# A gated mix of a long convolution and dilated attention: spectra regrouped in fours, inputs in transform rows, transposes on TensorE

## The chip, the cores and the metric

The kernel runs on one core of a Trainium2 chip. The metric is device time in microseconds (us) of one execution, lower is better. The engines are TensorE (PE in the profile; PEld are its weight loads), VectorE (DVE), ScalarE (ACT), GpSimd (POOL) and SyncE (SP). SP issues nearly all DMAs, in order, on one queue. A row "SPq" or "ACTq" of the profile is the issuing of a DMA on that engine's queue.

## The reference

The inputs are bf16: x, k, v of 2048 positions by 640 channels, and weights. The output mixes two branches by a gate per position.

```python
x = A_q
g = _sigmoid((x * gate_w).sum(-1, keepdims=True))
a = _A_ref(x, A_k, A_v, A_shift_k, A_ssm_k, A_ssm_D)
b = _B_ref(x, B_wqkv, B_wo)
return g * a + (1 - g) * b
```

Branch a convolves k with four taps per channel, multiplies by v (this is kv), convolves kv with a filter per channel as long as the sequence (`ssm_k`, by an FFT of length 4096), adds `kv * ssm_D` and multiplies by x. Branch b projects x to queries, keys and values of 32 heads of 20, attends from each position to the eight positions at distances 0, 2, ... 14 before it, and projects by `wo`.

## The kernel before, in words

All positions are split by parity into two halves of 1024, since the attention's distances are even. Branch b works on 18 blocks (9 a half) of 114 queries and 121 keys; a mask is added to the scores by 11 extra rows of the keys and queries, so a block's scores are a plain matmul, and an exponential on ScalarE makes the weights.

The order of the instructions on every engine comes from a planner (`Plan`, L149), which runs when the kernel is built. Each part of the kernel is a generator that asks for an engine with a cost in ns and the events it needs (`Req`); the planner starts whatever could start first, with 120 ns of handicap for each unit of the part's priority (the second argument of `plan.add`, L886 to L907). The costs and due times only fix the order; on the chip the engines wait on semaphores. Four pairs of PSUM banks are handed out by the planner (`take=1`). The helper `copy` (L273) empties PSUM on ScalarE (L275) or VectorE (L277), as the planner chooses.

The parts, in the order in which they matter:

- Loads (`loads`, L347): four DMAs that transpose x into `xT` (L355, channels on partitions), the weights of value, query and key, the taps, k and v in rows of 16 positions per partition (`kin`, `vin`), later `wo` and the filter `h_lin`.
- Value projection (`vproj`, L472) into `VW`, 18 units of 10 matmuls; query and key projection (`qkproj`, L516), 30 units into two staging tiles `stg`. `fragger` (L551) copies heads out of the staging tiles into three rotating sets `kb`, `qb` of four heads each, by 64 DMAs on SP (L573).
- Scores and weights (`score_gen`, L585; exponential at L604 into `ETall`) and the products with the values (`pv_gen`, L610), normalised by VectorE into `oS`.
- The short convolution (`conv`, L437): four taps and the product with v on VectorE, 4 positions of a partition at a time. Its result is written to DRAM (`kv_out`, L393), and read back (`kv_back`, L701) as `kvT`, which has 64 consecutive positions of 160 channels on each partition, the layout that the transform wants.
- The gate (`gate`, L492): 80 matmuls of one column, an exponential, then VectorE, then a write of 2048 numbers to DRAM (`g_scr`, L506) and four reads that turn them into `g_nat` (L509).
- The long convolution as a two-step transform (`transform`, L708): 10 first-step units (`s1_unit`, L649) and 11 second-step units (`s2_unit`, L669), each emptied by `copy`, in place. It is run for the filter (`h`) and for kv (`u`), each in two halves of 80 of the 160 channels of a partition group (P = 0, 1). In a spectrum tile the 40 channels of a group are innermost. A swapped copy `Hw` of the filter's spectrum (`swaps`, L740) lets VectorE form the complex product by two multiplications (`mults`, L756). `inverse1` (L773) is the first step back, 160 matmuls a half, into `Cm`.
- `outproj` (L794) turns `oS` (5 units of transposes), then multiplies by `wo` (16 units) and scales by 1 - g into `bl`.
- x is loaded again in rows (`late_loads`, L826), scaled by g on VectorE (`qscale`, L840), and `final` (L847) does the last step of the inverse in six rounds of up to 96 matmuls, multiplies, adds `bl` and stores.

Space decides much of the order. The second half of u takes the space of `oT`, so it follows the output projection (`ev("outproj")`, L735). `G`, the constants of the second step, takes the space of half of v, so it is loaded when the convolution and its writes are done (L402 to L407). `ETall` shares space with the taps (L309), so it waits for the first block of the convolution.

Of the kernel before, what the change touches and what calls it, by code (L numbers as in the profile page):

```python
# [10 lines left out]
BF = mybir.dt.bfloat16  # L11
# [22 lines left out]
XW = X0 + 2 * HS + 16  # L34
# [10 lines left out]
CR = 4  # L45
RES = 16
# [59 lines left out]
def ccol(sb):  # L106
    return X0 + 128 * sb


# [32 lines left out]
LEAN_QK = 600.0  # L142
LEAN_V = 0.0
LEAN_H = 0.0
# [103 lines left out]
def kernel(  # L248
# [39 lines left out]
    Wv = p0.tile([128, NDT, D], BF, name="Wv", tag="wo")  # L288
    kin = p0.tile([128, 16, D], BF, name="kin", tag="H")
    h_lin = p0.tile([128, 80, 2, 64], BF, name="h_lin", tag="kv")  # L290
# [3 lines left out]
    dpool = ctx.enter_context(tc.tile_pool(name="scratch_dram", bufs=1, space=DRAM))  # L294
    kv_d = dpool.tile([S, D], BF, name="kv_d")
    g_scr = dpool.tile([S], F32, name="g_scr")
    g_pos = p0.tile([128, 16], F32, name="g_pos")
    g_nat = p0.tile([128, 16], F32, name="g_nat")
    omg = p0.tile([128, 16], F32, name="omg")

# [8 lines left out]
    early = pR.tile([128, 3 * D + 4 * D], BF, name="early", tag="ET")  # L309
    halo = early[:, 0:3 * D].rearrange("p (n c) -> p n c", n=3)  # L310
    wraw = early[:, 3 * D:7 * D].rearrange("p (c j) -> p c j", j=4)
# [8 lines left out]
    pa = pL.tile([128, CR, D], BF, name="pa")  # L320
    pb = pL.tile([128, CR, D], BF, name="pb")
    wl = pL.tile([128, 4, D], BF, name="wl")
    mm = pL.tile([128, BK + BQ], BF, name="mm")
    Dz = pL.tile([128, 160], BF, name="Dz")
    wg = pL.tile([128, NDT], BF, name="wg")
# [17 lines left out]
    st = {"vin": [None, None]}  # L343

    def loads():  # L347
        def load(name, dst, src, us, deps=(), bg=None):
            g = yield Req("S", 500.0, deps, move=us, bg=bg, pri=None if bg is None else 1)
            nc.sync.dma_start(dst, src)  # L350
            mark(name, g)

        def load_x(c):
            g = yield Req("S", 500.0, (), move=2600.0)
            nc.sync.dma_start_transpose(xT[:, :, X0 + 512 * c:X0 + 512 * c + 512],  # L355
                                        raw(x2, (1024 * (c % 2) + c // 2) * D, [[2 * D, 512], [1, D]]))
            mark(f"x{c}", g)

        def load_rows(name, dst, src, r0, r1, deps=(), bg=1500.0):
            yield from load(name, dst, raw(src, r0 * D, [[16 * D, 128], [1, (r1 - r0) * D]]), (r1 - r0) * 128 * 1280 / 250.0, deps, bg)  # L360

        def load_k(a):
            yield from load_rows(f"k{a}", kin[:, 8 * a:8 * a + 8, :].rearrange("p n c -> p (n c)"), k2, 8 * a, 8 * a + 8)

        def load_v(a):
            v_ = p0.tile([128, 8, D], BF, name="vin", tag=("oS", "G")[a])
            st["vin"][a] = v_
            yield from load_rows(f"v{a}", v_[:].rearrange("p n c -> p (n c)"), v2, 8 * a, 8 * a + 8, ())

        yield from load_x(0)  # L370
        yield from load("Wv", Wv[:], W3[:, :, 2, :], 2600.0)
        yield from load_x(1)
        yield from load("W0", Wqk[:, :, 0, :], W3[:, :, 0, :], 2600.0)
        yield from load_x(2)
        yield from load("W1", Wqk[:, :, 1, :], W3[:, :, 1, :], 2600.0)
        yield from load_x(3)
        yield from load("wraw", wraw.rearrange("p c j -> p (c j)"), raw(A_shift_k, 0, [[0, 128], [1, 4 * D]]), 2200.0)
        for a, b in ((1, 113), (113, 128)):
            yield from load(f"halo{a}", halo[a:b].rearrange("p n c -> p (n c)"), raw(k2, (16 * a - 3) * D, [[16 * D, b - a], [1, 3 * D]]), 900.0)
        yield from load_k(0)  # L380
        yield from load_v(0)
        yield from load_k(1)
        yield from load_v(1)
        yield from load("ident", ident[:], ca["ident"].ap(), 200.0)
        wo = p0.tile([128, NDT, D], BF, name="wo", tag="wo")
        st["wo"] = wo
        yield from load("wo", wo[:], B_wo.rearrange("(t p) n -> p t n", p=128), 2400.0, [ev("vproj")], 1500.0)
        for c in range(2):
            for q in range(4):
                yield from load(f"h{q}{c}", h_lin[32 * q:32 * q + 32, :, c, :],  # L390
                                raw(A_ssm_k, (160 * q + 80 * c) * S, [[64, 32], [S, 80], [1, 64]]), 2100.0, (), 1500.0)

    def kv_out():  # L393
        for a in range(16 // CR):
            n = CR * a
            g = yield Req("S", 500.0, [ev(f"conv{a}")], move=2600.0)
            nc.sync.dma_start(raw(kv_d[0:1, 0:1], n * D, [[16 * D, 128], [1, CR * D]]),
                              st["vin"][n // 8][:, n % 8:n % 8 + CR, :].rearrange("p n c -> p (n c)"))
            mark(f"kvD{a}", g)

    def load_G():
        yield Req("S", 1.0, [ev("conv")])  # L402
# [7 lines left out]
    def heads():  # L410
        for c0, c1 in ((0, X0), (X0 + 2 * HS, XW)):
            nc.gpsimd.memset(xT[:, :, c0:c1], 0.0)
# [526 lines left out]
```

## Time and profile before

| | us |
|---|---|
| median of 3 runs | 282.11 |
| lowest and highest | 281.13, 284.21 |
| span of the profiled execution, first to last instruction | 280.1 |
| PE, DVE, ACT, POOL busy in it | 224.8, 175.6, 169.0, 20.2 |
| instructions | 8105 |

The profile is of one execution. Its own time is its span plus what lies before the first and after the last instruction, which the trace does not show; the median of the runs is 2.0 us above the span. A busy PE is not a PE at its full rate, as its matmuls overlap. 39.9 MB are moved by DMA. The convolution's last product on VectorE starts at 87.3 us, the last query/key unit at 131.7 and the last scores' exponential at about 155 us.

### The profile page before, as it was taken

How to read it: one execution, taken by the hardware profiler on the slowest of the kernel's cores; microseconds unless marked ns; L12 is line 12 of the kernel's file. 1: busy time of each engine (PE TensorE's matmuls, PEld its weight loads, DVE VectorE, ACT ScalarE, POOL GpSimd, SP SyncE). 2: the span in 40 equal slices, each digit the busy share in tenths (PEclk: the TensorE clock that was granted, in tenths of full speed). 3: DMA queues.
4: the chain of work that ended last, by engine and by line, in shares of the span. 5: the costliest groups of instructions: out<-in, count | busy, mean ns of one | idle time of the engine just before them, and what ended most of it. 6: DMA issues, size and time to landing. Idle time of an engine off the chain costs nothing.

```text
span 280.1 us, 8105 instructions
## 1 busy us (share of the span) xinstructions
PE 224.8 (80%) x3622; PEld 179.5 (64%) x3626; DVE 175.6 (63%) x186; ACT 169.0 (60%) x204; POOL 20.2 (7%) x23
## 2 busy tenths in 40 slices
PE   0699999699696985599899878989999979498420
PEld 0589787477454654456667867878977768398320
DVE  0012699999989533437787799999204266970682
ACT  1034256844877065368889798965765597166760
POOL 9940020000000000100000000000000000000000
PEclk9999999899877797579655799997999997779755
DMA  8999862976788438665699779000699940000275
GB/s 158 265 260 281 245 231 55 327 268 139 186 178 190 93 42 121 117 175 148 159 147 146 89 167 209 5 2 2 122 196 223 216 148 2 0 2 0 64 175 147
DMA packets 62857, 39.93 MB, mean 143 GB/s; under 512 B 52327, under 2 KB 59111, under 8 KB 61670
## 3 DMA queue, kind: packets, MB, share of 16 engines
q1 hardware_dynamic: 61870, 39.25, 62.0%
q8 instruction: 28, 0.46, 0.8%
q10 hardware_dynamic: 952, 0.16, 0.5%
q14 instruction: 7, 0.06, 0.1%
HBM read 20.87 MB, written 5.25 MB: 93 GB/s over the span
## 4 chain that ended last, share of the span: by engine, by line
PE 59%; DVE 12%; ACT 10%; DMA 8%; issue 5%; SPq 3%; ACTq 1%; DVEq 0%
PE pj L532 15%; PE i L783 10%; PE psv L481 10%; PE op L816 7%; ACT ETall L604 5%; DVE U L277 5%; PE s L676 5%; DMA g_scr<-g_pos 4%; PE sc L597 4%; PE O L624 3%; ACT U L275 3%; DMA Wv<-in_B_wqkv_dram 2%; PE i L865 2%; DMA h_lin<-in_A_ssm_k_dram 2%; DVE Hs L277 2%
## 5 line engine op out<-in xcount | busy, mean ns | idle before, releaser
L604 ACT ACTIVATE ETall<-sc 121x912 bf16<-121x912 f32 (+1 forms) x80 | 63.2, 858 | 22.2 <-PE sc L597 20.7
L532 PE MATMUL pj<-xT,Wqk 128*128 128x342 bf16 (+1 forms) x300 | 54.7, 335 | 2.0 <-DVE stg L277 0.9
L532 PEld LDWEIGHTS <-Wqk 128*128 128x128 bf16 x300 | 30.3, 104 | 19.5 <-issue 2.4
L277 DVE CAST stg<-pj 128x726 bf16<-128x726 f32 (+1 forms) x18 | 16.1, 894 | 35.1 <-PE pj L532 33.5
L481 PE MATMUL psv<-Wv,xT 128*121 128x320 bf16 x180 | 29.0, 317 | 10.0 <-DMA Wv<-in_B_wqkv_dram 9.7
L481 PEld LDWEIGHTS <-xT 128*121 128x121 bf16 x180 | 25.6, 143 | 11.5 <-POOL qb L423 7.5
L277 DVE CAST U<-s 128x1024 bf16<-128x1024 f32 (+2 forms) x23 | 25.9, 1168 | 10.7 <-ACT bl L820 7.3
L783 PE MATMUL i<-F,Hs 128*128 128x128 bf16 x160 | 28.6, 263 | 2.9 <-DVE Hs L766 2.9
L783 PE MATMUL i<-F,Hw 128*128 128x128 bf16 x160 | 28.4, 264 | 2.1 <-DVE Hw L769 2.1
L597 PE MATMUL sc<-qb,kb 31*128 31x114 bf16 x576 | 23.7, 240 | 8.0 <-ACT ETall L604 5.8
L275 ACT CAST Cm<-i 128x1024 bf16<-128x1024 f32 x20 | 20.2, 1012 | 14.0 <-PE i L783 14.0
L783 PEld LDWEIGHTS <-Hs 128*128 128x128 bf16 x160 | 26.4, 181 | 3.2 <-DVE Hs L766 3.1
L275 ACT CAST VW<-psv 121x640 bf16<-121x640 f32 x18 | 12.6, 698 | 26.3 <-PE psv L481 26.3
L783 PEld LDWEIGHTS <-Hw 128*128 128x128 bf16 x160 | 26.4, 182 | 2.3 <-DVE Hw L769 2.3
L275 ACT CAST Hs<-s 128x960 bf16<-128x960 f32 (+1 forms) x24 | 22.4, 1009 | 8.0 <-PE s L660 5.5
L597 PEld LDWEIGHTS <-kb 31*128 31x128 bf16 x576 | 14.1, 104 | 17.9 <-issue 17.0
L277 DVE CAST Hs<-s 128x1024 bf16<-128x1024 f32 (+2 forms) x18 | 20.5, 1152 | 7.2 <-PE s L660 5.0
L676 PEld LDWEIGHTS <-G 64*128 64x128 bf16 x512 | 22.0, 107 | 4.3 <-issue 2.7
L816 PE MATMUL op<-wo,oT 128*128 128x512 bf16 (+1 forms) x156 | 22.7, 302 | 1.1 <-ACT oT L275 0.9
L816 PEld LDWEIGHTS <-oT 128*128 128x128 bf16 x160 | 16.5, 147 | 6.9 <-ACT oT L275 1.2
L624 PEld LDWEIGHTS <-ETall 121*128 121x128 bf16 x576 | 17.2, 100 | 4.6 <-issue 2.9
L624 PE MATMUL O<-VW,ETall 121*128 121x21 bf16 x576 | 18.0, 176 | 2.4 <-ACT ETall L604 1.9
(54 smaller groups left out, 279.3 us busy)
## 6 DMA issues: line engine op xcount, KB each, us to landing
Hw<-Hs SPq DMA_DIRECT2D x8, 640.0 KB
kin<-in_A_k_dram SPq DMA_DIRECT2D x2, 1280.0 KB
vin<-in_A_v_dram SPq DMA_DIRECT2D x2, 1280.0 KB
kv_d<-vin SPq DMA_DIRECT2D x4, 640.0 KB
h_lin<-in_A_ssm_k_dram SPq DMA_DIRECT2D x8, 320.0 KB
kvT<-kv_d SPq DMA_DIRECT2D x8, 320.0 KB
qg<-in_A_q_dram SPq DMA_DIRECT2D x4, 640.0 KB
out_dram<-qg SPq DMA_DIRECT2D x20, 120.0 KB
```

The source lines that it names most:

```text
L275: nc.scalar.copy(dst, src)
L277: nc.vector.tensor_copy(dst, src)
L481: nc.tensor.matmul(ps[0:BK, n0 // 320, 0:320], lhsT=xT[:, dt, s0:s0 + BK], rhs=Wv[:, dt, n0:n1], start=(dt == 0), stop=(dt == NDT - 1))
L532: nc.tensor.matmul(ps[:, i, 0:n], lhsT=Wqk[:, dt, w, 128 * ft:128 * ft + 128], rhs=xT[:, dt, s0:s0 + n], start=(dt == 0), stop=(dt == NDT ...
L597: nc.tensor.matmul(sc[:, hh, BQ * bb:BQ * bb + BQ], lhsT=kb[r:r + DH + NF, BK * b:BK * b + 128], rhs=qb[r:r + DH + NF, BQ * b:BQ * b + BQ] ...
L604: nc.scalar.activation(st["ET"][0:BK, e, :, 0:BQ * nb], sc[0:BK, :, 0:BQ * nb], ACT.Exp, scale=SCALE)
L624: nc.tensor.matmul(O[:, (b - b0) // 6, c0:c0 + 21], lhsT=st["ET"][0:BK, e, hh, BQ * bb:BQ * bb + 128], rhs=VW[0:BK, b, 4 * t + h4, :], sta ...
L676: nc.tensor.matmul(ps[:, c, 160 * jj:160 * jj + 160], lhsT=st["G"][rows, j0 + jj, rr, :], rhs=Am[rows, :, 2 * (j0 + jj) + rr, :], start=(r ...
L783: nc.tensor.matmul(o, lhsT=src[:].rearrange("p q (j c) l -> p c l (q j)", c=2)[:, c, l + il, :], rhs=M[:, k, :], start=(k == 0), stop=(k = ...
L816: nc.tensor.matmul(op[:, n0:n1], lhsT=oT[:, ft].rearrange("p h m a -> p a (h m)")[:, t, :], rhs=wo[:, ft, n0:n1], start=(ft == 0), stop=(f ...
L865: nc.tensor.matmul(pss[q // 2][32 * gg:32 * gg + 32, q % 2, 160 * tt:160 * tt + 160], lhsT=T[rows, n2, r, :], rhs=Cm[rows, n2, r, :, :].re ...
```

## The change

It rewrites most of the parts, and keeps the mathematics.

- x is loaded plainly in eight pieces (`xn`) and turned by 80 transposes on PE into PSUM, each piece emptied by one copy (`xpose`).
- k and v are loaded at once in the transform's rows: 32 partitions for each group of 160 channels, 64 positions on each. The short convolution is done there: positions 8 to 63 on VectorE, in blocks of 8 positions, written over `kin`; positions 0 to 7 on GpSimd (`conv_g`). The product with v lands in `vin`, which the transform reads. The write to DRAM and the reading back are gone.
- The gate is computed as four rows of 512 on PE, one exponential on 128 by 512, four small copies from partition to partition into `g_nat`, then the arithmetic on VectorE. DRAM is not used.
- A spectrum's layout is now real/imaginary row, 10 groups, 128 frequencies, 4 channels: four channels are innermost in place of 40.
- Both halves of u are in one tile `UC`, which is also where the first inverse step puts its result. The second half of u no longer waits for the output projection. The inverse waits for all products of its half.
- `ETall` has space of its own. `G` and the first half of the filter's spectrum (`SX`) take the space of k and of the taps; the filter itself takes the space of `xn` and of the GpSimd part, so its loads, on SP, wait for that part (`convG`).
- x's second load goes into the space of the filter's first spectrum after the first inverse (`load_q`), and its scaling by g moves from VectorE to GpSimd.
- The constants T and `wo` are loaded when their own space opens; some first loads move to ScalarE's queue, five small ones to GpSimd's.
- The planner is the same; all priorities (`PRI`) and the three preferences for an engine (`LEAN_*`) are new. Both halves of each transform, product and inverse are streams of their own.

The core of the diff:

```diff
+PRI = dict(loads=0, fragger=0, xpose=1.5, score_gen=0.0, pv_gen=1.0, conv=3.0, conv_v=5.5, conv_g=0, conv_end=0, qkproj=2.1, vproj=2.7, gate=5.7,
+           load_G=0, h_slot=0, u_slot=0, swaps=0, load_T=0, op_tr=-7.6, outproj=14.1, load_q=0, qscale=0, final=3.6, h_stream=(6.3, 5.2),
+           u_stream=(10.8, 10.0), mults=(-3.3, 5.2), inverse1=(8.0, 7.7))
...
+        for c in (1, 0):
+            for q in range(4):
+                yield from load(f"k{q}{c}", kin[32 * q:32 * q + 32, 3 + 32 * c:35 + 32 * c, :], rows32(k2, q, 32 * c, 32 * c + 32), 1400.0, (), 1500.0)
+        for c in range(2):
+            for q in range(4):
+                yield from load(f"v{q}{c}", vin[32 * q:32 * q + 32, c], raw(v2, QC * q + 80 * c, [[64 * D, 32], [D, 64], [1, 80]]), 2050.0, (), 1500.0)
+        yield Req("S", 1.0, [ev("convG")])
+        h_lin = p0.tile([128, 80, 2, 64], BF, name="h_lin", tag="HL")
...
     def load_G():
-        yield Req("S", 1.0, [ev("conv")])
+        yield Req("S", 1.0, [ev("conv"), ev("grow"), ev("vproj")])
...
+    def xpose():
+        for a in range(8):
+            g = yield Req("P", 10 * 56.0, [ev(f"x{a}")], take=1, mode="f", mm=10)
+            tx = psum(g, "tx", (128, 2, HS), BF)
+            for e in range(2):
+                for dt in range(NDT):
+                    nc.tensor.transpose(tx[:, e, 128 * dt:128 * dt + 128], xn[:, a, e, 128 * dt:128 * dt + 128], ident[:])
+            r = yield Req("AD", dict(A=175.0 + 0.834 * 1280, D=140.0 + 0.54 * 1280), [g.done], give=g.banks)
...
+    def taps(eng, n, m, ta, tb, dst):
+        def tap(d, j):
+            w = wl[:, j, :].unsqueeze(1)
+            eng.tensor_tensor(d, kin[:, n + 3 - j:n + 3 - j + m, :], w.to_broadcast([128, m, QC]), ALU.mult)
+
+        tap(ta, 3)
+        for j in (2, 1, 0):
+            yield
+            tap(tb, j)
+            yield
+            eng.tensor_tensor(ta if j else dst, ta, tb, ALU.add)
...
+    def conv_g():
+        yield Req("G", 1.0, [ev("wl"), ev("xtr")] + [ev(f"k{q}0") for q in range(4)])
+        pgb = p0.tile([128, 2, GR, QC], BF, name="pgb", tag="HL")
+        c0 = 150.0 + 2.3 * GR * QC
+        yield Req("G", c0)
+        for _ in taps(nc.gpsimd, 0, GR, pgb[:, 0], pgb[:, 1], pgb[:, 0]):
+            yield Req("G", c0)
+        for c in range(2):
+            g = yield Req("G", c0 / 2, [ev(f"v{q}{c}") for q in range(4)])
+            vmul(nc.gpsimd, 0, GR, c, pgb[:, 0])
...
+        for dt in range(NDT):
+            for c in range(4):
+                o = X0 + HP * (c // 2) + 512 * (c % 2)
+                nc.tensor.matmul(gps[32 * c:32 * c + 32, :], lhsT=wgz[:, dt, :], rhs=xT[:, dt, o:o + 512],
+                                 start=(dt == 0), stop=(dt == NDT - 1), tile_position=(0, 32 * c), skip_group_check=True)
...
+        nc.scalar.activation(grow, gps[:], ACT.Exp, scale=-1.0)
...
+            nc.sync.dma_start(g_nat[32 * gg:32 * gg + 32, :], raw(src, 64 * (gg % 2) * pt + 16 * (gg // 2), [[32 * pt, 2], [32, 16], [1, 16]]))
...
-        copy(e.eng, Am[:, :, :, 4 * oc:4 * oc + 4].rearrange("p (a q) j l -> p a q j l", a=2),
-             ps[:].rearrange("p a (l q j) -> p a q j l", l=4, q=2))
+        copy(e.eng, Am[:, :, oc].rearrange("p r (a m) l -> p r a m l", a=2),
+             ps[:].rearrange("p a (l m r) -> p r a m l", l=4, r=2))
...
-                    nc.tensor.matmul(ps[:, c, 160 * jj:160 * jj + 160], lhsT=st["G"][rows, j0 + jj, rr, :], rhs=Am[rows, :, 2 * (j0 + jj) + rr, :],
+                    nc.tensor.matmul(ps[:, c, 160 * jj:160 * jj + 160], lhsT=st["G"][rows, j0 + jj, rr, :],
+                                     rhs=Am[rows, rr].rearrange("p o (q j) l -> p j (o q) l", j=32)[:, j0 + jj],
...
+    def u_slot():
+        yield Req("G", 1.0, [ev("pv"), ev("oS"), ev("p2")])
...
+        UC = st["p3"].tile([128, 2, 10240], BF, name="UC")
...
+    def inverse1(P):
+        yield Req("G", 1.0, [ev(f"mult{P}")])
...
+                    for k, key in enumerate("hw"):
+                        nc.tensor.matmul(d, lhsT=st[(key, P)][:, c, o + il // 4, :, il % 4], rhs=M[:, k, :],
...
     def qscale():
         for t in range(16):
-            r = yield Req("D", 230.0, [ev("qg"), ev("gate")])
+            r = yield Req("G", 700.0, [ev("qg"), ev("gate")])
             qg = st["qg"]
-            nc.vector.tensor_scalar(qg[:, t, :], qg[:, t, :], g_nat[:, t:t + 1], None, ALU.mult)
+            nc.gpsimd.tensor_scalar(qg[:, t, :], qg[:, t, :], g_nat[:, t:t + 1], None, ALU.mult)
```

More of the change, by code (lines that the diff above doesn't have):

```diff
@@ L341, in at @@
         ev(name).t = t
-    st = {"vin": [None, None]}
-    def loads():
[L348 to L368, printed above, removed]
+    st = {}
@@ L380, in loads @@
[L380 to L387, printed above, removed]
+        yield from load("W1", Wqk[:, :, 1, :], W3[:, :, 1, :], 3000.0)
+        for a in range(4, 8):
+            yield from load_x(a)
@@ L388, in loads @@
+        st["h_lin"] = h_lin
         for c in range(2):
@@ L711, in transform @@
         for oc in range(10):
-            d = yield from s1_unit(key, P, oc, Am, [])
+            d = yield from s1_unit(key, P, oc, Am)
             evs.append(d)
@@ L733, in u_stream @@
[L733 to L738 removed]
+        UC = st["p3"].tile([128, 2, 10240], BF, name="UC")
+        st["UC"] = UC
+        for P in range(2):
+            st[("u", P)] = UC[:, P].rearrange("p (c o m l) -> p c o m l", c=2, o=10, m=128)
+            st[("C", P)] = UC[:, P].rearrange("p (n r c l) -> p n r c l", n=64, r=2, c=2)
```

476 lines of the change are left out of this document (219 added, 257 removed).

## The prediction

> **What bounds the kernel now.** I read the summary first, then a table of stages, then the chain of waits between them, then the groups by shape. The chain that ended last has no owner: TensorE (PE) carries 59% of it and two engines 22%.
>
> ```profile
> PE 59%; DVE 12%; ACT 10%; DMA 8%; issue 5%; SPq 3%; ACTq 1%; DVEq 0%
> ```
>
> So I cut the span where the work changes. The columns after the window are its length, then busy us (instructions) of PE, PEld, DVE, ACT and POOL, then PE clock, DMA share and GB/s.
>
> ```profile
> 9.70:46.30 36.60, 36.60 (x250) 30.63 (x249) 17.91 (x17) 14.11 (x20) 10.12 (x9) 1.00 0.85 228
> 46.30:96.50 50.20, 42.42 (x651) 29.51 (x651) 45.32 (x44) 30.48 (x41) 0.00 (x0) 0.83 0.75 198
> 96.50:115.00 18.50, 11.51 (x189) 7.68 (x186) 6.46 (x10) 8.00 (x10) 0.94 (x1) 0.82 0.62 87
> ...
> 156.50:186.50 30.00, 26.83 (x577) 23.73 (x575) 27.36 (x27) 25.92 (x29) 0.00 (x0) 0.95 0.50 101
> 186.50:225.50 39.00, 37.20 (x332) 31.00 (x335) 16.09 (x25) 24.33 (x27) 0.00 (x0) 0.96 0.73 145
> 225.50:242.50 17.00, 10.62 (x203) 9.46 (x199) 13.32 (x12) 11.33 (x13) 0.00 (x0) 0.87 0.11 42
> 242.50:258.00 15.50, 14.35 (x159) 14.31 (x160) 7.87 (x6) 10.13 (x10) 0.00 (x0) 0.81 0.00 1
> ```
>
> Projections (9.7 to 46.3) are bound by PE; 46.3 to 96.5 by VectorE (45.3 of 50.2), which does the convolution; 96.5 to 115 by nobody; 156.5 to 186.5 by the two engines that empty PSUM (53.3 of 60); output projection and inverse by PE while VectorE rests; 225.5 to 242.5 again by the emptying engines. The chain of waits says why 96.5 to 115 is slow (start, length, what):
>
> ```profile
> 96.81 11.31 DMA g_scr<-g_pos
> 108.19 0.82 SPq L509
> ...
> 113.85 1.16 DMA kb<-stg
> 115.01 0.79 PE s L660 x8
> ```
>
> The gate's trip through DRAM holds SP's queue, with the copies of the next heads behind it. By shape (busy us, mean ns), these rows price the rest:
>
> ```profile
> L783 PEld LDWEIGHTS <-Hw 128*128 128x128 bf16 x160 | 26.4, 182 | 2.3 <-DVE Hw L769 2.3
> L816 PEld LDWEIGHTS <-oT 128*128 128x128 bf16 x160 | 16.5, 147 | 6.9 <-ACT oT L275 1.2
> L660 PEld LDWEIGHTS <-h_lin 64*128 64x128 bf16 x160 | 6.9, 110 | 8.0 <-POOL h_lin L687 4.4 <-issue 3.1
> L422 POOL COPY kb<-mm 128x2178 bf16<-128x2178 bf16 x3 | 6.0, 2001 | 0.1
> L687 POOL TENSOR_TENSOR h_lin<-h_lin,Dz 128x160 bf16<-128x160 bf16 x1 | 0.9, 943 | 73.9 <-DMA h_lin<-in_A_ssm_k_dram 73.9
> L445 DVE TENSOR_TENSOR pb<-kin,wl 128x1280 bf16<-128x1280 bf16 x1 | 0.8, 818 | 0.0
> ```
>
> Columns of weights 160 bytes apart (Hw) load in 182 ns, 32 bytes apart (oT) in 147, contiguous (h_lin) in 110.
>
> **The change part by part**, against the profiled execution's span of 280.1 us. The runs' median is 282.11, so 2.0 us lie around the span; I carry them.
>
> x turned by PE. Gone are four transposing loads, 2.9 + 2.6 + 4.7 + 5.3 = 15.5 us of SP's queue, and the first projection's wait until 9.66. Added are 8 plain loads, 80 transposes on PE at 57 ns (18 of oS took 1.02 us) = 4.5 us, and 8 evictions of 1280 bf16: the 2048 form took 1.22 us, so about 0.8, 6.4 us on VectorE, hidden by its 18.7 idle us of 9.7 to 46.3; uncovered they would lengthen the start by their first one. I take 2 us off the start and 4.5 onto PE, which is full there: +2.5 (bounds -5, if PE waits for x anyway, and +6).
>
> Convolution in transform rows. Gone: 49.7 us on VectorE (28 taps and sums of up to 1.49, 4 products, one copy of 1.49). Added: 7 blocks by 7 operations of 818 ns = 40.1, 4 products of 2240 elements at 1.32 (between 1.15 at 1920 and 1.49 at 2560) and a small copy: 45.9. POOL gets the last eighth: 7 operations of 1280 elements and two half ones, 8 in all. No row has POOL with two dense operands. The copy's 0.92 ns per element gives 1.2 us, L687's 943 ns for 160 widely spaced elements gives 7.5 (5.9 ns per element); I take twice the copy, 2.4, because two streams are read and both are dense: 19 us. What that does to VectorE no row shows, since POOL ran while VectorE had little to do. Bounds -4 (VectorE's saved work) and +19 (VectorE stands while POOL works); I take +6, near the middle, because VectorE was busy 45.3 of 50.2 us where this falls. Behind POOL's products stand the 8 loads of h, which wait in SP's queue in front of copies for later heads.
>
> k and v without DRAM. Gone are four writes of kv and eight reads back, the reads 16.5 us of SP's queue (138.9 to 155.4). Added: k and v in 8 loads each. v's have the reads' 160-byte runs, 2.1 us of SP each, 17 us in the first 60. They replace the 15.5 of the transposing loads, so 0 (bounds -5 and +10: head copies are queued behind them).
>
> Queues. ACT's list of DMAs at the start grows from 7 to 16, at about 0.45 us each 7.2 us, then the 1.28 table load; its first work was at 12.5, so nothing. Uncovered, 4 us. POOL issues 5 small DMAs behind its memsets, needed only by the gate and by D's sum: nothing.
>
> Gate. 80 matmuls (2.0 us) become 20, the transfer of 11.3 us becomes four small ones between partitions, the chain on VectorE stays three small operations. SP still waits for an exponential that comes behind others on ScalarE, with head copies behind it. The saving lies between the 4.3 us for which PE waited on the kb copy and the 11.3 of the transfer; I take -8, as PE was busy 11.5 of the 18.5 us.
>
> Scores sooner. ETall has space of its own and query/key goes ahead of value on PE, so scores can start before 46.3, when ScalarE was busy 14.1 of 36.6 us. Bounds 0 and -10; I take -4, since PE is full.
>
> Both halves resident. The second transform of kv leaves 225.8 to 239.1 (13.3 us on the chain) and goes to where the second transform of h was, in 156.5 to 186.5; h's must then go ahead, into 96.5 to 156.5, where the emptying engines have 43 idle us (200% of 60 less 77.2 busy) for its 22.6 (21 evictions of about 1.08). Output projection, 21 us of PE, fills the products' time. -13.3 (bounds 0, if h's does not fit, and -20). The products' lead before the second inverse (239.1 to 242.5) goes too: -3.5. What is late next is the product on VectorE, 23.8 us for both halves.
>
> Spectra in fours. The inverse's weights are now 8 bytes apart instead of 160. Its 320 matmuls took 14.1 + 14.4 us, 88 ns each; transposes, 18 in 1.02 us with contiguous weights, cost 57. I take 56: 17.9 us, -10.6. Bounds 0 (as 160 bytes) and -10.6 (as contiguous). Eviction then needs both engines: 10 of 1.01 us on ScalarE alone would outlast 9 us of PE. Reading moving operands in runs of four has no row; at worst it would stretch 512 second-stage matmuls of 37 ns. I take nothing, as they are paced by evictions.
> The Trainium skill (SBUF — State Buffer, Specifications (TRN2)) says a line is 16 bytes and that two hits in it are needed for full bandwidth. By that rule 8-byte columns are as good as contiguous (-10.6); the trace agrees in direction (182, 147, 110 ns) and has no row at 8 bytes.
>
> q's scaling. 16 x 381 ns leave VectorE, which was idle; POOL gets 16 x 640 elements at the copy's rate, 9.4 us, after a load that last took 16 us (197.8 to 213.8) and now starts only after the first inverse. The second inverse and the products (9 and 12 us) cover most: +2 (bounds 0 and +14). The final stage (258 to 280) stays.
>
> Sum: 2.5 + 6 - 8 - 4 - 13.3 - 3.5 - 10.6 + 2 = -28.9; 280.1 - 28.9 + 2.0 = **253 us**.
>
> **The rivals.**
> (A) POOL stops VectorE. If an operation on POOL and one of VectorE with two SBUF operands exclude each other, VectorE loses 19 us instead of 6 in its fullest stage: +13, 266 us. For it: POOL's share is set in the middle of VectorE's convolution. Against: conv ended at 88.8 and G was issued only at 119.9, so 31 us of slack exist.
> The Trainium skill (SBUF — State Buffer, Who interferes with whom) states just this exclusion; no run here shows it yet.
> (B) The change does not do what it says at the weights: the load stays at 182 ns and the inverse at the 82 ns that it had at full clock. 320 x 26 ns = +8.3, 261 us.
> (C) Slower: POOL at L687's rate. Eight operations of 7.5 us are 60 us where the planner's formula for POOL (150 + 2.3 x 1280 ns) gives 25. SP then stands 35 us at the loads of h, head copies behind it, and attention stops: 253 + 35 = 288. It decides from 54 us of POOL work on, 5.3 ns per element. Against: h_lin's elements are 256 bytes apart, these are dense.
> (D) Better: POOL costs nothing and its share is a gain (-10 against the sum), q hides (-2), scores -6 instead of -4: 239. For it: from 46.3 to 156.5 PE's work is about 77 us of 110 (200 pj at 149 ns, 576 sc at 36, 576 O at 26, the rest 12).
>
> **How the numbers follow.** Forecast 0.36 (own range 246 to 260), A 0.20, B 0.12, C 0.14, D 0.18. Range 238 to 277: it reaches from D to A with B's price on top (266 + 8) and a little over, and leaves C and few others out. A measurement of this kernel tells about 1% from no change. Faster by over 1%: 0.36 + 0.18 + 0.12 + 0.16 of A = 0.82; within 1%: 0.04, A at its worst; slower: C, 0.14.
>
> **What would show it.** Inverse: weight loads near 110 ns and 0.9 us per 16 matmuls; B if they stay at 182. Gate: no wait of over 3 us on SP for it. Halves: no stretch after output projection with only transform evictions. POOL: its operations near 2.4 us and VectorE's 1280-element ones still at 0.82; A if those have gaps or grow beside POOL. SP: waits for POOL before h's loads under 5 us; C if they are tens. If PE still stands at the copies of heads between 46 and 156, or the final stage waits for q, I am wrong there.

## The result, and the profile after

The changed kernel takes 298.26 us (median of 4 runs, 297.04 to 300.68) against 281.62 for the kernel before (4 runs): a ratio of 1.057, 95% interval 1.050 to 1.065. It is slower by nearly 6%; 253 was forecast. The profiled execution took 300.68 us, its span is 298.9.

I cut both spans at two marks that every version has: the start of the last normalisation of the attention, and the start of the last matmul of the inverse.

| us | to the last normalisation | to the end of the inverse | rest | span |
|---|---|---|---|---|
| before | 156.9 | 99.8 | 23.4 | 280.1 |
| forecast (its terms sorted by stage) | 153.4 | 72.4 | 25.4 | 251.2 |
| after | 162.3 | 86.7 | 49.9 | 298.9 |

Of the 47.7 us between the forecast span and the real one, 8.9 are missing in the first stretch, 14.3 in the second, 24.5 in the last. The chain that ended last now belongs to GpSimd (POOL) more than to any engine but TensorE (PE), and it is short:

```profile
PE 14%; POOL 9%; DMA 5%; issue 3%; DVE 2%; POOLq 1%; SPq 0%
```

The table of stages of the changed kernel (length, busy us and instructions of PE, PEld, DVE, ACT and POOL, PE clock, DMA share, GB/s), cut at the first transposes, first scores, first step of the filter's transform, end of the last normalisation, and both ends of the inverse:

```profile
4.10:57.30 53.20, 41.88 (x311) 35.35 (x312) 34.72 (x29) 11.51 (x16) 38.98 (x24) 0.95 0.96 185
57.30:136.40 79.10, 70.50 (x1022) 45.46 (x1023) 68.30 (x93) 44.37 (x56) 5.17 (x4) 0.88 0.75 113
136.40:163.00 26.60, 23.83 (x528) 18.21 (x527) 22.11 (x28) 23.49 (x30) 0.00 (x0) 0.52 0.34 100
163.00:231.20 68.20, 59.81 (x938) 48.46 (x945) 57.47 (x48) 49.61 (x58) 0.00 (x0) 0.94 0.42 94
231.20:249.20 18.00, 18.00 (x323) 18.00 (x322) 7.33 (x6) 13.97 (x15) 0.00 (x0) 1.00 0.20 40
249.20:298.90 49.70, 8.24 (x522) 5.97 (x521) 18.65 (x13) 10.86 (x14) 30.79 (x16) 0.58 0.43 93
```

Three things to see. In the first row PE, which was full in 9.7 to 46.3 before, is busy 41.9 of 53.2 us, and POOL is busy 39. The fifth row is the inverse, both halves without a gap, 18.0 us for 320 matmuls. In the last row POOL is the busiest, with 30.8 of 49.7 us. The chain of waits through it (start, length, what):

```profile
231.37 13.41 PE i L791 x240
244.78 0.30 SPq L841
...
246.19 14.27 DMA SX<-in_A_q_dram
...
262.59 8.45 POOL SX L848 x4
...
272.90 16.75 POOL SX L848 x9
...
289.67 1.76 DVE SX L881
```

x's second load is issued when 240 of the 320 inverse matmuls are through and lands 15.7 us later; only then do POOL's 16 scalings run, 31 us that the multiplications and stores of the last step wait for. The groups by shape that answer to the forecast's prices (busy us, mean ns | idle before and its releaser):

```profile
L848 POOL TENSOR_SCALAR SX<-SX,g_nat 128x640 bf16<-128x640 bf16 x16 | 30.8, 1939 | 138.5 <-DMA SX<-in_A_q_dram 138.5
L791 PEld LDWEIGHTS <-Hw 128*128 128x128 bf16 x160 | 17.9, 114 | 0.0
L454 POOL TENSOR_TENSOR pgb<-KX 128x1280 bf16<-128x1280 bf16 x4 | 12.1, 3043 | 10.1 <-DMA qb<-stg 9.9
...
L454 DVE TENSOR_TENSOR KX<-KX 128x1280 bf16<-128x1280 bf16 x28 | 30.9, 1116 | 2.1 <-DMA g_nat<-KX 1.8
L461 DVE TENSOR_TENSOR KX<-KX 128x1280 bf16<-128x1280 bf16 x21 | 23.4, 1114 | 1.3 <-DMA g_nat<-KX 0.9
```

A scaling costs 1.94 us on POOL (3.0 ns per element; the copy, 0.92, was the price taken). The inverse's weights load in 114 ns where they took 182. And VectorE's (DVE) 49 convolution operations, 818 ns each when undisturbed, have a mean of 1115: 54.3 us in place of 40.1 (49 x 0.818). The mean hides two kinds. Here is the order of time on DVE while POOL has its seven operations (37.0 to 58.7); columns are start, length, instruction:

```profile
36.57 0.82 DVE L454 TENSOR_TENSOR KX<-KX 128x1280 bf16<-128x1280 bf16 x1
37.42 3.12 DVE L461 TENSOR_TENSOR KX<-KX 128x1280 bf16<-128x1280 bf16 x1
40.46 0.90 DVE L278 CAST stg<-pj 128x726 bf16<-128x726 f32 x1
41.29 5.55 DVE L454 TENSOR_TENSOR KX<-KX 128x1280 bf16<-128x1280 bf16 x2
...
50.01 3.11 DVE L454 TENSOR_TENSOR KX<-KX 128x1280 bf16<-128x1280 bf16 x1
53.16 3.10 DVE L461 TENSOR_TENSOR KX<-KX 128x1280 bf16<-128x1280 bf16 x1
```

A tap or sum lasts up to as long as POOL's operation beside it (3.04), while a cast out of PSUM keeps its 0.90. The casts are not stretched, but they are queued behind the taps, and SP's copies of heads wait for the casts: 9.0 us before the first scores, 6.8 of it at once, up to 47.7 (in e4 below, SP waits 3.8 us for VectorE up to the same time). The first scores come at 57.3 in place of 46.3, and a wait of 9.3 us for a sum follows them.

### The profile page after: what moved, and what is told of

Its sections match the earlier page's. It is cut to its first block, busy times and chain, and to the rows that moved or that the text cites. A ratio compares the mean times of both kernels' runs of the same rounds, so it can differ in the third digit from the quotient of the medians.

```text
span 298.9 us, 8211 instructions
## 1 busy us (share of the span) xinstructions
PE 222.3 (74%) x3639; PEld 171.5 (57%) x3646; DVE 208.6 (70%) x214; ACT 153.8 (51%) x186; POOL 77.9 (26%) x57
## 5 line engine op out<-in xcount | busy, mean ns | idle before, releaser
L848 POOL TENSOR_SCALAR SX<-SX,g_nat 128x640 bf16<-128x640 bf16 x16 | 30.8, 1939 | 138.5 <-DMA SX<-in_A_q_dram 138.5
L618 PE MATMUL sc<-qb,kb 31*128 31x114 bf16 x576 | 24.1, 246 | 14.1 <-DMA vin<-in_A_v_dram 4.9
L278 DVE CAST stg<-pj 128x684 bf16<-128x684 f32 (+1 forms) x30 | 26.6, 888 | 9.0 <-PE pj L557 4.5
L510 PE MATMUL psv<-KX,xT 128*121 128x320 bf16 x180 | 30.4, 323 | 2.9 <-ACT VW L276 1.9
L454 DVE TENSOR_TENSOR KX<-KX 128x1280 bf16<-128x1280 bf16 x28 | 30.9, 1116 | 2.1 <-DMA g_nat<-KX 1.8
L881 DVE TENSOR_TENSOR SX<-yb,SX 128x1920 bf16<-128x1920 bf16 (+1 forms) x6 | 9.2, 1538 | 25.4 <-POOL SX L848 25.4
L276 ACT CAST UC<-s 128x960 bf16<-128x960 f32 (+2 forms) x25 | 22.4, 966 | 8.2 <-PE s L695 8.0
L695 PEld LDWEIGHTS <-SX 64*128 64x128 bf16 x512 | 20.0, 98 | 10.7 <-issue 9.6
L825 PE MATMUL op<-wo,oT 128*128 128x512 bf16 (+1 forms) x153 | 24.5, 312 | 0.4
L461 DVE TENSOR_TENSOR KX<-KX 128x1280 bf16<-128x1280 bf16 x21 | 23.4, 1114 | 1.3 <-DMA g_nat<-KX 0.9
L876 ACT CAST yb<-i 128x960 bf16<-128x960 f32 (+1 forms) x12 | 9.9, 873 | 25.4 <-DVE SX L881 17.8
L278 DVE CAST UC<-s 128x1024 bf16<-128x1024 f32 (+1 forms) x17 | 19.3, 1193 | 4.1 <-PE s L695 3.3
L278 DVE CAST SX<-s 128x1024 bf16<-128x1024 f32 (+1 forms) x15 | 17.1, 1187 | 1.7 <-PE s L679 1.6
```

The source lines that it names most:

```text
L276: nc.scalar.copy(dst, src)
L278: nc.vector.tensor_copy(dst, src)
L454: eng.tensor_tensor(d, kin[:, n + 3 - j:n + 3 - j + m, :], w.to_broadcast([128, m, QC]), ALU.mult)
L461: eng.tensor_tensor(ta if j else dst, ta, tb, ALU.add)
L510: nc.tensor.matmul(ps[0:BK, n0 // 320, 0:320], lhsT=xT[:, dt, s0:s0 + BK], rhs=Wv[:, dt, n0:n1], start=(dt == 0), stop=(dt == NDT - 1))
L618: nc.tensor.matmul(sc[:, hh, BQ * bb:BQ * bb + BQ], lhsT=kb[r:r + DH + NF, BK * b:BK * b + 128], rhs=qb[r:r + DH + NF, BQ * b:BQ * b + BQ] ...
```

## The experiments

Theory: the loss has two causes on POOL. (1) q's scaling stands alone at the end, because its load waits for the inverse and POOL is slow at it. (2) POOL's share of the convolution stops VectorE. Rivals: for the first, that the late load alone is the cost, or POOL's slowness alone; for the second, that the new order of the work delays the scores, POOL or not. After these runs a third question was left: why both resident halves gave so little. Every run's spans, cut as above (e10 and e6 were run once; the other times are medians, and the ratios are to the kernel before on the same chip). The three stretches are those of the one profiled execution, which for e3 was its fastest (273.35 us):

| version | us | ratio to before, 95% interval | to last norm. | inverse | rest |
|---|---|---|---|---|---|
| after | 298.3 | 1.057 (1.050 to 1.065) | 162.3 | 86.7 | 49.9 |
| e1, q scaled on DVE | 284.1 | 1.002 (0.997 to 1.006) | 162.8 | 84.5 | 34.4 |
| e2, q loaded early | 275.5 | 0.973 (0.966 to 0.980) | 161.8 | 86.9 | 25.2 |
| e3, both | 275.9 | 0.966 (0.956 to 0.976) | 160.7 | 85.6 | 24.4 |
| e4, convolution on DVE | 282.3 | 0.994 (0.989 to 1.000) | 151.7 | 81.4 | 48.6 |
| e5, e3 and e4 | 264.0 | 0.929 (0.921 to 0.936) | 152.3 | 83.6 | 26.1 |
| e6, POOL writes only | 286.7 | - | 148.1 | 86.8 | 50.0 |
| e7, before, q scaled on POOL | 285.1 | 1.002 (0.998 to 1.006) | 161.2 | 99.1 | 24.1 |
| e8, e5, casts on ScalarE | 270.8 | 0.952 (0.944 to 0.960) | 160.9 | 83.8 | 24.2 |
| e9, e5, scaling after products | 259.8 | 0.917 (0.912 to 0.922) | 151.3 | 81.1 | 25.8 |
| e10, e1 with a quarter of q | 272.8 | - | 160.8 | 84.3 | 25.4 |
| e11, e9, filter's transform first | 265.1 | 0.933 (0.928 to 0.938) | 173.8 | 65.5 | 25.2 |

Two profiles of the same work differ: e7 runs the instructions of the kernel before in the same order up to the scaling, and its first stretch is 161.2 us against 156.9. Those of after, e1, e2, e3 and e10 lie between 160.7 and 162.8.

**q's scaling: e1, e2, e3, e7.** e1 moves it to VectorE, after the same late load:

```diff
-            r = yield Req("G", 700.0, [ev("qg"), ev("gate")])
+            r = yield Req("D", 300.0, [ev("qg"), ev("gate")])
-            nc.gpsimd.tensor_scalar(qg[:, t, :], qg[:, t, :], g_nat[:, t:t + 1], None, ALU.mult)
+            nc.vector.tensor_scalar(qg[:, t, :], qg[:, t, :], g_nat[:, t:t + 1], None, ALU.mult)
```

> The changed kernel with one line moved: q's scaling runs on VectorE again; load and everything else stay. Theory 1 (the end is set by the late load of q and by GpSimd's 16 scalings of 1.9 us): the load still lands near 260, 16 scalings take 5 us in place of 30.8, then the rounds and the stores take about 18, so the time falls by about 14 us, to 284. Theory 2 (the loss is made early, where GpSimd's share of the convolution stops VectorE, and the end only follows): less than 5 us faster. Theory 3 (the new order loses): no more than 5 us faster as well.

e2 leaves the scaling on POOL, and loads 12 of the 16 groups of positions into the space of `G` as soon as the last second step of u has read it, the other 4 after the first inverse:

```diff
-        yield Req("S", 1.0, [ev("i10")])
-        qg = st["SX"][:, 0:16 * D].rearrange("p (t n) -> p t n", t=16)
...
+        for e, t0, m, o, need in ((0, 0, 12, 10240, ("us20", "us21")), (1, 12, 4, 0, ("i10",))):
+            yield Req("S", 1.0, [ev(x) for x in need])
+            qg = st["SX"][:, o:o + m * D].rearrange("p (t n) -> p t n", t=m)
...
```

> The changed kernel with q loaded earlier: rows 0 to 11 of each partition go into G's space as soon as both second steps of u are done (about 215 us), rows 12 to 15 as before after the first inverse; the scaling stays on GpSimd. Theory 1: GpSimd starts near 230, its first 12 scalings of 1.9 us are done near 253 while the inverses run, the last four near 260, so the rounds start near 251 and the time falls by 20 to 24 us, to about 276. If only GpSimd's rate matters and not the load: a fall of less than 12. Theories 2 and 3: less than 5.

e3 does both.

> Both: q loaded earlier as in the run before, scaled on VectorE. Theory 1: the final stage takes the 22 us that it takes in the kernel before, counted from the end of the second inverse (250 us): 272 us of span, about 274 in all, 24 us less than the changed kernel. If the final stage has another bound (instructions of PE arriving late): above 280.

The last stretch is the answer: 49.9 (late, POOL), 34.4 (late, VectorE), 25.2 (early, POOL), 24.4 (early, VectorE), 23.4 before. The group of scalings in e1 (busy us, mean ns | idle before):

```profile
L848 DVE TENSOR_SCALAR SX<-SX,g_nat 128x640 bf16<-128x640 bf16 x16 | 4.8, 379 | 10.2 <-DMA SX<-in_A_q_dram 10.2
```

The same group in e2, on POOL, hidden behind the products and the inverse:

```profile
L849 POOL TENSOR_SCALAR SX<-SX,g_nat 128x640 bf16<-128x640 bf16 x16 | 36.1, 2266 | 105.1 <-PE op L825 105.1
```

The slow scaling costs 15.5 us after a late load and 0.8 after an early one, though it is slower still there (2.27 us each); the 0.8 is no more than the other versions with an early load differ among themselves (24.2 to 26.1). The late load costs 10.0 with VectorE's scaling. So neither rival holds alone: together they cost 25.5, and apart 10.0 and 0.8. e7 asks the same of the kernel before, whose load is early, by giving its scaling to POOL:

```diff
-                nc.vector.tensor_scalar(qg[:, t, :], qg[:, t, :], g_nat[:, t:t + 1], None, ALU.mult)
+                nc.gpsimd.tensor_scalar(qg[:, t, :], qg[:, t, :], g_nat[:, t:t + 1], None, ALU.mult)
```

> The kernel before with one line moved: q's scaling on GpSimd. There q has landed by 214 us and the final stage starts at 258. Theory 1 (slow scalings hurt only because q comes late): 16 of 1.9 us run from 214 to 245 behind the output projection, stop some of VectorE's products (239 to 250) for 2 to 5 us, and the time stays within 2% of before. If GpSimd's rate alone is the loss: slower by 10 us or more.

It is the same time within 0.6% (1.002), with the scalings on POOL:

```profile
L844 POOL TENSOR_SCALAR qg<-qg,g_nat 128x640 bf16<-128x640 bf16 x16 | 34.4, 2174 | 99.2 <-ACT bl L820 99.2
```

Three of the six products that VectorE runs beside them last 0.5 to 0.7 us longer than in the kernel before, 1.8 us in all, and it does not show in the time.

**The convolution: e4, e6.** e4 gives POOL's eighth of the convolution back to VectorE.

```diff
-GR = 8
+GR = 0
...
-            for n in range(GR, 64, 28):
+            for n in range(GR, 64, 32):
...
-        for _ in taps(nc.gpsimd, 0, GR, pgb[:, 0], pgb[:, 1], pgb[:, 0]):
-            yield Req("G", c0)
-        for c in range(2):
-            g = yield Req("G", c0 / 2, [ev(f"v{q}{c}") for q in range(4)])
-            vmul(nc.gpsimd, 0, GR, c, pgb[:, 0])
```

> The changed kernel with the whole convolution on VectorE (all 64 positions), nothing of it on GpSimd; q's scaling as in the changed kernel. If GpSimd's operations stop VectorE's operations with two SBUF operands (rival A of the prediction, theory 2): VectorE's 3.1 us operations between 37 and 58 us fall back to 0.82, 20 us of stops go, 6 us of work come, scores start 10 us sooner than 57, and the time falls by 8 to 14 us, to about 287. If there is slack behind it, less than 4 us faster. If VectorE's own 6 us weigh more: slower by up to 6.

The ratio falls from 1.057 to 0.994, by more than expected. With an eighth more work, VectorE spends less on it (56 operations, 45.5 us, against 54.3 for 49). The taps of e4, busy us and mean ns:

```profile
L454 DVE TENSOR_TENSOR KX<-KX 128x1280 bf16<-128x1280 bf16 x32 | 25.8, 818 | 3.4 <-DMA g_nat<-KX 3.1
```

The first scores come at 47.1, and the last normalisation 10.6 us sooner. The other 6.6 us of the 17.2 by which the span is shorter lie behind it. There e4 also has another order of instructions, since the planner plans anew, and what of the 6.6 us is due to that was not tried. All of it would also follow if POOL's results were simply late, so e6 keeps VectorE's part and replaces POOL's seven operations by 21 memsets of the same tile, which write SBUF and read none. It leaves out the taps of positions 0 to 7. The order of the instructions on VectorE, ScalarE and TensorE stays that of after.

```diff
-        for _ in taps(nc.gpsimd, 0, GR, pgb[:, 0], pgb[:, 1], pgb[:, 0]):
+        for i in range(7):
+            for _ in range(3):
+                nc.gpsimd.memset(pgb[:, i % 2], 0.0)
```

> The changed kernel with GpSimd's seven tap operations replaced by 21 memsets of the same space, which only write SBUF and take about as long (the taps of positions 0 to 7 are left out). If VectorE's operations with two SBUF operands wait only for a GpSimd operation that reads SBUF: VectorE's operations at L454 and L461 stay at 0.82 us while GpSimd is busy, as with the convolution on VectorE, and the time falls by 10 to 16 us. If any GpSimd operation stops them: they stay at 3 us and the time at 298.

POOL is busy for 25 us (21.7 with the taps and sums), and VectorE does not notice; it does when POOL comes to its product, which reads SBUF. POOL in e6 in order of time (start, length, instruction):

```profile
29.18 24.90 POOL L492 MEMSET pgb<- 128x1280 bf16 x21 [2.62 <-PE tx L440]
54.91 1.95 POOL L465 TENSOR_TENSOR vin<-pgb,vin 128x640 bf16<-128x640 bf16 x1 [0.83 <-DMA vin<-in_A_v_dram]
```

VectorE in e6 at the same times, two taps beside the memsets and two beside the product:

```profile
46.95 1.55 DVE L454 TENSOR_TENSOR KX<-KX 128x1280 bf16<-128x1280 bf16 x2
...
54.79 2.75 DVE L454 TENSOR_TENSOR KX<-KX 128x1280 bf16<-128x1280 bf16 x2
```

The last normalisation comes at 148.1, 14.2 us sooner, and the stops counted above are 54.3 - 40.1 = 14.2 us; that the two agree to the tenth is luck, as two profiles of the same work differ by more. So it is the reading that stops VectorE, not the new order, which e6 keeps; and SP waited only 0.4 us for POOL in after, so it is not POOL's being late either. The Trainium skill (SBUF — State Buffer, Who interferes with whom) says so: a VectorE instruction with two SBUF inputs contends with a GpSimd instruction that reads SBUF and not with one that only writes it. Both halves of that sentence are seen here (3.1 us beside a read, 0.78 beside a memset).

It is not always VectorE that stands. In e2, POOL's first scaling starts among VectorE's products, which follow each other without a gap and keep their 1.48 us. The scaling lasts 5.88 us where 1.87 is usual, and ends 1.8 us after the last product:

```profile
226.91 5.88 POOL L849 TENSOR_SCALAR SX<-SX,g_nat 128x640 bf16<-128x640 bf16 x1 [105.13 <-PE op L825]
...
228.15 1.48 DVE L779 TENSOR_TENSOR Hs<-UC,Hs 128x2560 bf16<-128x2560 bf16 x1
229.55 1.48 DVE L779 TENSOR_TENSOR Hw<-UC,Hw 128x2560 bf16<-128x2560 bf16 x1
```

The taps and sums, each of which needs the one before, stand 0.03 us apart, and there VectorE was the one to wait. That the gaps decide it was not tried.

**Both together: e5.** The edits of e3 and e4.

> The changed kernel with q loaded early, q scaled on VectorE and the whole convolution on VectorE. If the two losses are separate (the late q: 298 to 276; GpSimd's share of the convolution: 298 to 282), they add up: 276 - 16 = 260 us, faster than the kernel before by 8%. If one hides behind the other: above 268.

The losses add: 7% faster than before. In its trace 12 scalings (3.6 us; the expectation of e9 below has 11) stand on VectorE ahead of the last four products of the second half, behind a wait of 2.5 us for q's load, and that half's inverse waits 1.7 us. e9 puts the scalings behind the products:

```diff
-            r = yield Req("D", 300.0, [ev(f"qg{t // 12}"), ev("gate")])
+            r = yield Req("D", 300.0, [ev(f"qg{t // 12}"), ev("gate"), ev("mult1")])
```

> The same version (264.0 us), with q's scaling put behind the last product of the second half on VectorE. In it 11 scalings (3.2 us) stand between the products of the second half, whose inverse begins 1.7 us after the first ends. If that wait is what they cost, the second inverse follows the first without a gap and the time falls by about 2 us (below 1%, hardly to be told in the time, so the gap in the trace is what counts); if it lengthens the final stage instead, no change or 1 to 3 us more.

The gap is gone: from the first inverse matmul at 214.5 to the last at 232.4 it is 17.9 us. At 259.75 us, 8.3% faster than before, it is the fastest version of the study. The ratios of e5 and e9 differ by 1.2 points, and their intervals just overlap (0.921 to 0.922).

**Where the resident halves' gain went: e8, e11.** In e9 the second stretch is 18.7 us shorter than before, of which the faster inverse is 10.6; the forecast had 27.4. Before, the filter's transform began at 115; in the versions so far it begins at 134 to 137, behind a convolution that ends at about 130 (88.8 before). Only in e6, whose convolution ends at 117, does it begin at 122, and its second stretch is no shorter for that (86.8). Part of the convolution's delay is VectorE's casts of the query and key projections, of which the change gives it all 30 (instructions of the tile `stg` in after; shortest/median/longest ns, first and last start):

```profile
L278 DVE CAST stg<-pj x30: 857/886/917, 20.1 to 134.2; 128x684 bf16<-128x684 f32 x15, 128x726 bf16<-128x726 f32 x15
```

In the kernel before, 18 were on VectorE and 12 on ScalarE:

```profile
L277 DVE CAST stg<-pj x18: 860/910/916, 18.3 to 132.1; 128x726 bf16<-128x726 f32 x10, 128x684 bf16<-128x684 f32 x8
L275 ACT CAST stg<-pj x12: 729/730/844, 26.6 to 80.6; 128x684 bf16<-128x684 f32 x7, 128x726 bf16<-128x726 f32 x5
```

e8 is e5 with 29 of them on ScalarE:

```diff
-LEAN_QK = 1040.0
+LEAN_QK = 0.0
```

> The version with q early, q's scaling and the whole convolution on VectorE (264.0 us on another chip, against 284.1 of before), with one number changed: the handicap of ScalarE for emptying the query and key projections goes from 1040 to 0 ns, so that the planner gives it nearly all 30 casts in place of none. They were 26.6 us of VectorE, among which the convolution ended at 130 and the filter's transform began at 135, while ScalarE was busy 63 of the 110 us from 20 to 130. Theory 1 (both halves resident gained little because the late convolution kept the filter's transform behind the attention): the convolution ends near 80, the transform begins near 100, and the time falls by 8 to 12 us, to 252 to 256. Theory 2 (there was no room: what emptying and matmuls move forward the attention pays, since exponentials and casts then queue on ScalarE): the transform begins near 100 as well, the last normalisation comes 8 to 12 us later than 151, and the time stays within 1% of 264 or goes up to 272.

The convolution ends at 92.9 and the transform's first step begins at 111.4, but attention ends 8.6 us later than in e5 and the stretch after it is as long (83.8 and 83.6). The second step still came after the attention, so this did not test the forecast's idea in full. e11 does, on top of e9:

```diff
-           ... h_stream=(6.3, 5.2),
+           ... h_stream=(0.0, 0.0),
```

> The version with q early, its scaling on VectorE behind the last product and the convolution on VectorE (259.75 us), with the priority of the filter's transform raised: both its halves, first and second steps, go ahead of the scores as soon as the convolution is done. With the casts on ScalarE the first step began at 111 in place of 135, but the second step still came after the attention, so that run did not yet do what the forecast meant. Theory 1 (the late place of the filter's transform is what both resident halves did not give): the second step ends before the last normalisation, the stretch from that to the end of the second inverse shrinks from 81 to about 65 us, attention ends at most 5 us later than 151, and the time falls to 245 to 252. Theory 2 (no room: the attention pays for what goes ahead of it): the stretch shrinks to about 65 as well, but the last normalisation comes 16 us or more later, at 167 or after, and the time is 258 to 268.

The whole transform now lies ahead of the last normalisation (second steps of both its halves in e11, columns as above):

```profile
L688 PE MATMUL s<-SX x128: 226/227/332, 144.5 to 155.5; 64*128 64x160 bf16 x128
L688 PE MATMUL s<-Hs,SX x128: 226/227/240, 152.3 to 160.2; 64*128 64x160 bf16 x128
```

The normalisations of e11:

```profile
L651 DVE TENSOR_TENSOR oS<-O,rd x24: 647/657/658, 60.8 to 173.8; 114x480 bf16<-114x480 f32 x24
```

The stretch after shrinks to 65.5 us, as the forecast wanted, and the attention ends 22.5 us later. Two windows of e9, from 133 to the last normalisation and on to the end of the inverse, columns as in the table of stages:

```profile
133.00:151.30 18.30, 16.64 (x381) 12.76 (x379) 15.01 (x19) 15.81 (x21) 0.00 (x0) 0.50 0.51 172
151.30:232.60 81.30, 73.32 (x1276) 63.22 (x1276) 69.96 (x71) 65.25 (x74) 0.00 (x0) 0.99 0.52 112
```

The same two of e11:

```profile
133.00:173.80 40.80, 35.08 (x719) 27.90 (x720) 30.98 (x35) 34.51 (x40) 0.00 (x0) 0.71 0.25 83
173.80:239.50 65.70, 63.82 (x958) 55.76 (x961) 56.14 (x58) 48.97 (x55) 0.00 (x0) 0.96 0.62 137
```

In e9's first window PE is busy 91% of the time: it leaves little room. The 318 instructions that e11 takes out of the second window saved 9.5 us of PE's busy time there and, with 20 others, added 18.4 to the first, where the granted clock was 0.50 (0.71 with them). That the lower clock is why the trade loses is argued from this, not shown.

**A wait of TensorE's own: e10.** In e1 PE stood 7.9 us, from 250.5 to 258.4, waiting for no semaphore, while the load of q ran (in after from 252.2 to 260.1). e10 is e1 with a quarter of the load:

```diff
-            nc.sync.dma_start(qg[32 * g:32 * g + 32], raw(x2, (32 * (g // 2) + g % 2) * D, [[64 * D, 32], [2 * D, 16], [1, D]]))
+            nc.sync.dma_start(qg[32 * g:32 * g + 32, 0:4], raw(x2, (32 * (g // 2) + g % 2) * D, [[64 * D, 32], [2 * D, 4], [1, D]]))
```

> The changed kernel with q's scaling on VectorE (284.1 us), and q's load cut to the first 4 of its 16 position groups; the other 12 are left as they were in memory, so a part of the output is not computed. In the last stage TensorE waited 7.9 us for its own instructions (no semaphore) while the load of 2.6 MB ran. Theory 1 (the load on all DMA engines delays the fetch of TensorE's instructions): the wait falls to 2 to 3 us and the load's 16 us to about 4; the span falls by 8 to 12 us, to about 271. Theory 2 (TensorE's instructions of that stage are late in any case): the wait stays at 7 to 8 us, and the span falls by 5 us at most.

PE's waits in the last step of the inverse, us in total, times, longest, in e1:

```profile
PE i L869 <- issue: 10.0, 2, 7.9
```

The same in e10:

```profile
PE i L869 <- issue: 5.4, 3, 2.4
```

The long wait is gone; the total fell to 5.4 and not to 2 or 3, which is near the kernel before (4.8, longest 1.9). The span is 11.2 us shorter, 9.0 of it in the last stretch, but not because of PE: in e1 VectorE waited for q until 259.0, after PE had gone on, and in e10 its scalings start at 246.5. Nor is the load enough to make PE's wait long. e4 has the same late load of 2.6 MB (issued at 227.0, landed at 242.9) and waits no longer than e10:

```profile
PE i L862 <- issue: 5.2, 3, 2.3
```

What PE waits for can be read from the trace's list of DMA packets, of which the page shows the totals: queue q8, "instruction", has 28 packets of 16 KB, one for some 260 of PE's matmuls and weight loads. In the 13 versions PE has 32 waits of over 0.7 us of this kind in the last step, and each ends 1.2 to 1.6 us after such a packet has arrived. In e1 the packet moves from 255.6 to 257.0, 13.7 us after the one before it (13.7 in after and 13.6 in e6 too); in e10, 8.3 us after; in e4, 12.7 us after (222.0 to 234.6). So beside the full load the packet is late in e4 too, but most of that falls into the inverse, where PE still had instructions. PE waits for its instructions, and the load delays them; how long PE then stands depends on what it still has to do.

## Why the prediction was wrong, point by point

- **q's scaling, +2: failed, 26.5** (the last stretch, 49.9 against 23.4). The step that failed is "The second inverse and the products (9 and 12 us) cover most". The products of both halves were done when the inverse began, but for the last (231.2 and 232.4), and its halves ran into each other: the load was issued with 80 matmuls, some 4 us, left. The price failed too ("at the copy's rate, 9.4 us": 30.8). It lies between the two rows that I had for POOL, 0.92 and 5.9 ns per element, and I took the cheap one as if it were known; the upper bound of 14 fell short for the same reason.
- **POOL's share of the convolution, +6: mis-sized, 14 to 17** (14.0 is the span of after less that of e6, where only the stops are gone; 17.2 is that of after less that of e4, 298.9 - 281.7, with another order behind the attention). POOL's operation came out inside its bounds (2.4 us taken, 3.04 measured); what it does to VectorE was taken in the middle, and it is near the top. Rival A had the mechanism. Its counterargument, 31 us of slack behind the convolution, failed: the loss does not go through the convolution's end but through the casts between the taps, for which the copies of heads wait. VectorE was also fuller than the sum had it, by 12 more casts (30 x 0.89 less the 16.1 us of before, 10.5 us, from one of the new preferences, which I did not cost). How much that adds was not tried with POOL's share in place.
- **Both halves resident, -13.3, and the products' lead, -3.5: failed, -2.5 in after** (99.8 - 86.7 less the inverse's 10.6), -8.1 in e9. The step was "h's must then go ahead, into 96.5 to 156.5", with 43 idle us of the emptying engines counted. It did not go ahead, and when e11 makes it, the attention pays 22.5 us for the 15.6 that the later stretch saves. My bound "0, if h's does not fit" was the right case. I counted the emptying engines' idle time of the old order and not PE's at its clock there.
- **Spectra in fours, -10.6: right in mechanism and size** (17.9 us for 320, 56 ns each), though a part is luck. The 88 ns were taken at a lower granted clock (0.81 in the second inverse before) than the inverse after has (1.00). With the 82 ns of full clock that rival B names, the layout is worth 320 x 26 ns = 8.3 us, and the other 2.3 are the clock, which the sum took along unsaid. Rival B falls. The Trainium skill's lines of 16 bytes with two hits (SBUF — State Buffer, Specifications (TRN2)) agree: weights 8 bytes apart load in 114 ns, where 160 apart took 182. That rule does not tell 32 bytes apart (147) from 160, as both have one hit a line.
- **Gate, -8: its wait is gone** (SP's longest for it is 1.5 us); what that is worth was not tried by itself.
- **Scores sooner, -4: failed.** 57.3 in after, and 47.1 in e4, against 46.3 before: PE is full from 20 to 50 in e4, so there was little to gain.
- **Queues, 0: nearly.** ScalarE's list of DMAs ran to 13.3 us, not 7.2; PE waited 1.9 us for the first eviction. x turned by PE (+2.5) was not tried by itself.
- **Rival C, the slower one, did not occur** in its place (SP waited 0.4 us for POOL at the loads of h). The kernel was slower by a mechanism that was in my sum with +2.

Without POOL's two costs and the late load, e9's span is 258.2, 7.0 above the forecast's 251.2, and the terms say why: the halves give 8.7 less, the first stretch 3.9 less (5.6 us in place of the 9.5 of x, gate and scores), the last 0.4 less, and the +6 for POOL is gone. What is open: how the 5.6 us that e9 gains up to the last normalisation divide among gate, x and queues (and how large they are, as the same work took 4.3 us more in e7's profile than in that of before); and whether some order can use the resident halves.

## What to carry to other kernels

Moving work to a slower engine is free only as long as its input is early: look for the instruction that releases the load, count what still runs after that instruction, and price the operation from a row of the same kind on the same engine, or take its bound at the dearest row. Before GpSimd shares elementwise work, ask what VectorE reads beside it: where VectorE had two operands in SBUF, an eighth of its work given away cost 14 us. Work moved ahead into a stage must find idle time on every engine that it uses, in the new order and at the clock granted there.

## What was not expected of the hardware

- A VectorE operation with both operands in SBUF and a GpSimd operation that reads SBUF hold each other up. Between dependent taps it was VectorE's that waited (818 ns becomes 3.1 us), beside products without a gap it was GpSimd's (1.87 us becomes 5.88). A VectorE cast out of PSUM does not change (0.90), and a GpSimd memset stops neither.
- GpSimd scales a 128 by 640 bf16 tile by a number per partition in 1.94 us with VectorE nearly idle, 2.17 to 2.27 with it busy; VectorE does so in 0.38.
- TensorE can stand for its own instructions. Beside a load of 2.6 MB a 16 KB packet of the instruction queue came 12.7 to 13.7 us after the one before, beside a quarter of the load 8.3. TensorE's longest wait for one was 7.9 us, in the last step of the inverse, and 2.3 where most of the delay fell into an earlier step.
